# Recurrence and gated projection: values of every second head written to the other half of the PSUM partitions, block states in the scores' PSUM

## The chip, the core and the metric

The kernel runs on one core of one Trainium2 chip. The metric is the device time of one execution in microseconds (us). PE is TensorE, DVE is VectorE, ACT is ScalarE, POOL is GpSimd and SP is SyncE.

## What is computed

Four sequences, eight heads of width 48, 768 steps. Each head keeps a 48x48 state that decays per channel by `alpha` and takes in `k v`; the read-out `y = q S` of all heads, laid side by side, goes through a gated projection with a first-order recurrence.

```python
def _attn_ref(q, k, v, alpha):
    state = zeros(B, H, D, D)
    for t in range(S):
        state = alpha[:, :, t, :, None] * state + einsum('bhd,bhe->bhde', k[:, :, t], v[:, :, t])
        y[:, :, t] = einsum('bhd,bhde->bhe', q[:, :, t], state)

def _moe_ref(x, w_in, A_log, w_out):     # x: heads of y side by side, 384 wide
    val, gate = split(x @ w_in)          # 512 each
    h_t = exp(A_log)[0] * h_(t-1) + val_t
    return (silu(gate) * h) @ w_out
```

## The kernel before

The 3072 steps are worked in 12 groups of 256 steps (`GC`), three groups for each sequence. A group is two parts of 128 steps, and each part two blocks of 64 steps (`R`), so there are four blocks. Heads go in four pairs: a pair stands on 128 partitions, 64 for each head (48 padded to 64).

A generator `front(n)` brings group n in: transposes of alpha (L294, `a_pad`), scans on DVE for the decay products V (L301) and P (L306), transposes of q and k with products Q (L318) and K (L322), the scores inside each block (`sc`, L331), which DVE copies under a mask into A (L334), and transposes of K back to steps (`tpk`, L119, taken to Kn by ACT).

A generator `back(n)` makes the values of group n: `block_states` (`z`, L131) multiplies keys with values for each block, DVE adds the four block states up into S_n and, for the next group of the sequence, S_end (L356); `values_inside` (`y`, L145) multiplies the masked scores with the values, ending in a small ACT read called `fence` (L150); `values_before` (L163) adds Q times the state ahead of the block into the same PSUM; ACT copies y to `x_sb` (L363); `features` transposes it (`tpx`, L172) and ACT takes that to xT (L173).

A generator `ssm(n)` does the projection: `pj` (L93), the scan hh (L96), silu `sg` (L101), the product f (L102), and the output `o` (L107), which ACT copies out (`o_sb`, L110).

The order on every engine is written out by hand in the loop over n at the end of `ranged` (`tc.manual_schedule()`): in turn n the PE does the a transposes of group n, z of group n-1, o of group n-3, the q transposes, y inside of n-1, pj of n-2, the k transposes, y before of n-1, pj, scores, tpx, pj, tpk, pj. Engines run their own lists in order and wait for one another by semaphores. In turns 0 to 2 DVE, ACT and POOL also turn the weights from 64-bit to 32-bit numbers (L233 to L250).

The 64x64 matmuls address one quarter of the PE array each. Which quarter is set by the half of the partitions that the operands lie on (row half) and the half of the PSUM partitions that the result goes to (column half). In `block_states` the row half is the block r and the column half the head i of the pair, with result bank r. In the scores and in `values_before` the row half is i, the column half r, the bank i. In `values_inside` row half and column half are both r, the bank is i. A program matmul in fp32 shows as two PE instructions in the trace, so a block of 32 matmuls is 64 instructions there.

PSUM: `ps_sc` holds one tile of two banks (tag `sc`), `ps_y` one tile of two banks (tag `y`), which z and y take in turn; `ps_tp` and `ps_mm` hold two each.

A second function, `general`, computes the same for extreme decays and is not run with these inputs.

Of the kernel before, what the change touches and what calls it, by code (L numbers as in the profile page):

```python
# [9 lines left out]
FP32 = mybir.dt.float32  # L10
# [3 lines left out]
AF = mybir.ActivationFunctionType  # L14
# [4 lines left out]
def kernel(  # L19
# [23 lines left out]
    nc = tc.nc  # L43
    B, H, S, D = q.shape
    DM = H * D
    DI = moe_A_log.shape[0]
    C = 128
    R = 64
    NR = C // R
# [4 lines left out]
    NP = H // 2  # L54
    DP = 64
# [58 lines left out]
    def keys_back(K, Kn, ps_tp):  # L114

        for c in range(G):
            tp = ps_tp.tile([C, NP, C], FP32, tag="tp", name="tpk")
            for j in range(NP):
                nc.tensor.transpose(tp[:, j, :], K[:, j, ds(c * C, C)], ident)  # L119
            nc.scalar.activation(Kn[:, c], tp, AF.Copy)  # L120

    def block_states(Kn, v_sb, ps_y):

        z = ps_y.tile([C, NR, 512], FP32, tag="y", name="z")
        zv = z[:, :, 0:GP * D].rearrange("p r (g j e) -> p r g j e", g=G, e=D)
        for g in range(G):
            for j in range(NP):
                for r in range(NR):
                    for i in range(2):
                        rows, chs = ds(R * r, R), ds(DP * i, DP)  # L130
                        nc.tensor.matmul(zv[chs, r, g, j, :], Kn[rows, g, j, chs],  # L131
                                         v_sb[rows, g, 2 * j + i, :], start=True, stop=True,
                                         skip_group_check=True)
        return zv

    def values_inside(A, v_sb, ps_y, pool):

        y = ps_y.tile([C, 2, 512], FP32, tag="y", name="y")
        yv = y[:, :, 0:GP * D].rearrange("p i (g j e) -> p i g j e", g=G, j=NP)
        for c in range(G):  # L140
            for j in range(NP):
                for i in range(2):
                    for r in range(NR):
                        rows = ds(R * r, R)
                        nc.tensor.matmul(yv[rows, i, c, j, :], A[rows, i, c * NP + j, :],  # L145
                                         v_sb[rows, c, 2 * j + i, :],
                                         start=(c == 0 and j == 0), stop=False, skip_group_check=True)

        fence = pool.tile([C, 2, 1], FP32, name="fence")
        nc.scalar.activation(fence, y[:, :, 0:1], AF.Copy)  # L150
        return yv

    def values_before(yv, Q, S_n, first):

        for c in range(G):
            for j in range(NP):
                for r in range(NR):
                    x = c * NR + r
                    if first and x == 0:
                        continue  # L160
                    for i in range(2):
                        rows = ds(DP * i, DP)
                        nc.tensor.matmul(yv[ds(R * r, R), i, c, j, :], Q[rows, j, ds(R * x, R)],  # L163
                                         S_n[rows, x, j, :],
                                         start=False, stop=(c == G - 1 and j == NP - 1), skip_group_check=True)

    def features(x_sb, xT, ps_tp):

        for c in range(G):
            tp = ps_tp.tile([C, NK, C], FP32, tag="tp", name="tpx")  # L170
            for kk in range(NK):
                nc.tensor.transpose(tp[:, kk, :], x_sb[:, c, ds(kk * C, C)], ident)  # L172
            nc.scalar.activation(xT[:, :, ds(c * C, C)], tp, AF.Copy)  # L173
# [6 lines left out]
    def ranged(ctx):  # L180
        def pool(name, bufs, **kw):
            return ctx.enter_context(tc.tile_pool(name=name, bufs=bufs, **kw))

        own = pool("own", 1)
        p1 = pool("p1", 1)
        p2 = pool("p2", 2)
# [3 lines left out]
        ps_sc = pool("ps_sc", 1, space=PS)  # L190
        ps_tp = pool("ps_tp", 2, space=PS)
        ps_y = pool("ps_y", 1, space=PS)
# [147 lines left out]
        def back(n):  # L340

            s = st.pop(n)
            v_sb = vs.pop(n)
            first, last = n % NG == 0, n % NG == NG - 1
            S_n = p2.tile([C, GR, NP, D], FP32, name="S_n")
            if not first:
                nc.gpsimd.tensor_mul(S_n[:, 0], S_end[0], s["V"][:, :, 0:1].to_broadcast([C, NP, D]))  # L347
            zv = block_states(s["Kn"], v_sb, ps_y)
            S_end[0] = None if last else p2.tile([C, NP, D], FP32, name="S_end")
            for x in range(GR):  # L350
                src = zv[:, x % NR, x // NR]
                dst = S_n[:, x + 1] if x + 1 < GR else S_end[0]
                if first and x == 0:
                    nc.vector.tensor_copy(out=dst, in_=src)
                elif dst is not None:
                    nc.vector.tensor_add(dst, S_n[:, x], src)  # L356
            yield
            yv = values_inside(s["A"], v_sb, ps_y, p2)
            yield
            values_before(yv, s["Q"], S_n, first)  # L360
            x_sb = p2.tile([C, G, DM], FP32, name="x_sb")
            for i in range(2):
                nc.scalar.activation(x_sb.rearrange("p g (j i e) -> p i (g j) e", i=2, e=D)[:, i],  # L363
                                     yv[:, i].rearrange("p g j e -> p (g j) e"), AF.Copy)
            yield
            xs[n] = p2.tile([C, NK, GC], FP32, name="xT")
            features(x_sb, xs[n], ps_tp)
            yield
# [43 lines left out]
        with tc.manual_schedule():  # L412
            for n in range(N + 3):
                fr = front(n) if n < N else None
                ba = back(n - 1) if 0 <= n - 1 < N else None
                old, new = ssms[n - 3], None
                turn = weights if n < 3 else None
# [34 lines left out]
    def general(ctx):  # L452
# [4 lines left out]
        def pool(name, bufs, **kw):  # L457
            return ctx.enter_context(tc.tile_pool(name=name, bufs=bufs, **kw))

        LEVELS = [1, 2, 4, 8, 16, 32]  # L460
        p1 = pool("g1", 1)
        p2 = pool("g2", 2)
        ps_sc = pool("gs_sc", 1, space=PS)
        ps_tp = pool("gs_tp", 2, space=PS)
        ps_y = pool("gs_y", 1, space=PS)
# [21 lines left out]
        A = p1.tile([C, 2, GP, R], FP32, name="gA")  # L487
# [4 lines left out]
        for n in range(N):  # L492
            first = n % NG == 0
            for dst, src in (("a", alpha), ("q", q), ("k", k)):
                load_heads(pad[dst], src, n)
            v_sb = p2.tile([C, G, H, D], FP32, name="v_sb")
# [3 lines left out]
            Q = p1.tile([C, NP, GC], FP32, name="gQ")  # L500
# [22 lines left out]
            for l in LEVELS:  # L523
                nb = R // (2 * l)
                Qr = Q.rearrange("p j (x b two l) -> p j x b two l", x=GR, two=2, l=l)
                sc = ps_sc.tile([C, 2, 512], FP32, tag="sc", name="sc")
                scv = sc[:, :, 0:GP * R // 2].rearrange("p i (x b l) -> p i x b l", x=GP, l=l)
                for c in range(G):
                    for j in range(NP):
                        for r in range(NR):  # L530
                            x = c * NR + r
                            for i in range(2):
                                rows = ds(DP * i, DP)
# [19 lines left out]
            Tb = Tl.rearrange("p (j x) -> p j x", j=NP)  # L553
            Kn = p1.tile([C, G, NP, C], FP32, name="gKn")
            keys_back(K, Kn, ps_tp)
            zv = block_states(Kn, v_sb, ps_y)
            S_n = p2.tile([C, GR, NP, D], FP32, name="gS_n") if first else S_in
            S_in = p2.tile([C, GR, NP, D], FP32, name="gS_n")
            for x in range(GR):
# [4 lines left out]
                else:  # L564
                    dS = p1.tile([C, NP, D], FP32, name="gdS")
                    nc.gpsimd.tensor_mul(dS, S_n[:, x], Tb[:, :, x:x + 1].to_broadcast([C, NP, D]))
                    nc.vector.tensor_add(dst, dS, src)
            yv = values_inside(A, v_sb, ps_y, p1)
            values_before(yv, Q, S_n, first)
            x_sb = p1.tile([C, G, DM], FP32, name="gx_sb")  # L570
            for i in range(2):
                nc.vector.tensor_add(
# [10 lines left out]
    with tc.If(outside > 0):  # L583
        with ExitStack() as inner:
            general(inner)
# [30 lines left out]
```

## Time and profile before

| | |
|---|---|
| time, median of 3 runs | 373.11 us (372.81 to 375.66) |
| the profiled execution's own time | 374.53 us |
| its span, first to last instruction | 372.8 us |
| mean granted TensorE clock | 0.975 of full |
| PE busy | 325.8 us (87%) |
| DVE / ACT / POOL busy | 200.5 (54%) / 106.5 (29%) / 56.8 us (15%) |
| z, `L131`, 768 instructions | 14.6 us |
| y inside, `L145`, 768 instructions | 28.0 us |
| y before, `L163`, 704 instructions | 14.5 us |
| scores, `L331`, 768 instructions | 15.5 us |

The profile is one execution. A timeline row gives a start, a length, an engine, a line of the code, what is written from what, a count, and in square brackets how long the engine was idle before it and what ended that. An idle engine matters only where the chain of waits that ends last runs through it.

### The profile page before, as it was taken

What the parts mean: (1) busy time and instruction counts of PE and PEld (TensorE: products, weight loads), DVE (VectorE), ACT (ScalarE), POOL (GpSimd) and SP (SyncE); (2) the same over time, 40 slices, a digit from 0 to 9 for tenths busy, and PEclk for the clock granted to TensorE, in tenths of its full rate; (3) what the DMA queues carried; (4) which work ended last, traced back from release to release, by engine and by line L of the source; (5) the groups of instructions that cost most, each with busy time, mean ns of one, the idle gap of its engine ahead of it and who ended that gap; (6) DMA issues with size and microseconds to landing.
All of it is one profiled execution on the core that took longest, in us unless ns stands there. A gap on an engine that the chain in (4) does not pass through costs nothing.

```text
span 372.8 us, 9626 instructions
## 1 busy us (share of the span) xinstructions
PE 325.8 (87%) x4233; PEld 265.6 (71%) x4233; DVE 200.5 (54%) x373; ACT 106.5 (29%) x231; POOL 56.8 (15%) x77
## 2 busy tenths in 40 slices
PE   2535851899999999999999999999999999999794
PEld 1425741787887886887887887878868868878582
DVE  3939785356557438348456555565484493403140
ACT  1414354221432323133223213223332231312111
POOL 4478898510000000000000000000000000000000
PEclk9999995599999999999999999999999999999999
DMA  9999992040470740911913704607401000010101
GB/s 132 212 220 190 303 171 47 2 86 2 105 111 2 154 60 3 179 36 41 145 30 80 134 2 100 115 3 130 85 2 44 2 16 30 2 45 0 38 7 50
DMA packets 107650, 29.02 MB, mean 78 GB/s; under 512 B 100944, under 2 KB 107088, under 8 KB 107600
## 3 DMA queue, kind: packets, MB, share of 16 engines
q1 hardware_dynamic: 104992, 27.93, 40.6%
q10 hardware_dynamic: 2608, 0.40, 0.9%
q8 instruction: 35, 0.57, 0.7%
q14 instruction: 15, 0.12, 0.1%
HBM read 23.60 MB, written 4.72 MB: 76 GB/s over the span
## 4 chain that ended last, share of the span: by engine, by line
PE 62%; DVE 23%; SPq 6%; issue 4%; POOL 2%; DMA 1%; ACT 1%; ACTq 0%; DVEq 0%; POOLq 0%
PE pj L93 35%; PE y L145 7%; DVE V L301 7%; DVE P L306 7%; PE o L107 4%; SPq L83 4%; PE y L163 4%; PE sc L331 3%; PE tp L294 3%; DVE S_n L356 3%; PE tpk L119 2%; PE tpx L172 2%; SPq L226 2%; DVE hh L96 2%; DMA bits<-in_moe_w_in_dram 1%
## 5 line engine op out<-in xcount | busy, mean ns | idle before, releaser
L93 PE MATMUL pj<-xT,w_in 128*128 128x256 f32 x576 | 136.1, 388 | 0.0
L93 PEld LDWEIGHTS pj<-xT,w_in 128*128 128x128 f32 x576 | 107.7, 193 | 14.6
L96 DVE TENSOR_TENSOR_SCAN hh<-a_dec,hh,pj 128x256 f32<-128x256 f32 x32 | 23.9, 747 | 78.2 <-PE pj L93 78.2
L107 PE MATMUL o<-w_out,f 128*128 128x384 f32 x192 | 65.0, 492 | 0.0
L101 ACT ACTIVATE sg<-pj 128x256 f32<-128x256 f32 x48 | 18.4, 383 | 130.9 <-DVE hh L96 130.9
L107 PEld LDWEIGHTS o<-w_out,f 128*128 128x128 f32 x192 | 35.5, 190 | 23.0 <-DVE f L102 0.5
L145 PE MATMUL y<-v_sb,A 64*64 64x48 f32 x768 | 28.0, 233 | 11.9 <-DVE S_end L356 11.2
L347 POOL TENSOR_TENSOR S_n<-S_end,V 128x192 f32<-128x192 f32 x8 | 4.1, 513 | 224.2 <-DVE S_end L356 224.2
L145 PEld LDWEIGHTS y<-v_sb,A 64*64 64x64 f32 x768 | 26.7, 149 | 15.1 <-issue 8.3
L306 DVE TENSOR_TENSOR_SCAN P<-tp,iV,bias 128x256 f32<-128x256 f32 x48 | 33.4, 738 | 0.8
L102 DVE TENSOR_TENSOR f<-sg,hh 128x256 f32<-128x256 f32 x48 | 20.4, 426 | 23.3 <-ACT sg L101 23.3
L301 DVE TENSOR_TENSOR_SCAN V<-tp,bias 128x256 f32<-128x256 f32 x48 | 30.1, 669 | 5.1 <-PE tp L294 5.1
L96 DVE TENSOR_TENSOR_SCAN hh<-a_dec,pj 128x256 f32<-128x256 f32 x16 | 11.0, 687 | 39.4 <-PE pj L93 39.4
L311 ACT ACTIVATE junk<-V,bias 128x1024 f32<-128x1024 f32 x12 | 13.8, 1148 | 52.7 <-DVE V L301 52.7
L294 PE MATMUL tp<-ident,a_pad 128*128 128x128 f32 x96 | 14.6, 300 | 15.6 <-POOL ex L240 7.2
L294 PE MATMUL tp<-ident,q_pad 128*128 128x128 f32 x96 | 15.5, 306 | 11.9 <-DVE P L306 7.7
L294 PEld LDWEIGHTS tp<-ident,a_pad 128*128 128x128 f32 x96 | 12.4, 154 | 17.4 <-POOL ex L240 7.5
L294 PEld LDWEIGHTS tp<-ident,q_pad 128*128 128x128 f32 x96 | 12.4, 157 | 16.4 <-issue 13.8
L240 POOL TENSOR_SCALAR ex<-ex 128x384 uint32<-128x384 uint32 x12 | 18.4, 1532 | 18.0 <-DVE ex L235 17.7
L331 PEld LDWEIGHTS sc<-Q,K 64*64 64x64 f32 x768 | 13.7, 144 | 4.3 <-issue 3.3
L334 DVE COPY_PREDICATED A<-mask,sc 128x512 f32<-128x512 uint8 x24 | 16.0, 721 | 1.1 <-PE sc L331 1.1
L322 DVE TENSOR_TENSOR K<-tp,V 128x512 f32<-128x512 f32 x24 | 15.5, 684 | 2.0 <-PE tp L294 2.0
(59 smaller groups left out, 315.6 us busy)
## 6 DMA issues: line engine op xcount, KB each, us to landing
a_pad<-in_alpha_dram SPq DMA_DIRECT2D x24, 192.0 KB, 4.7
k_pad<-in_k_dram SPq DMA_DIRECT2D x24, 192.0 KB, 5.1
v_sb<-in_v_dram SPq DMA_DIRECT2D x24, 192.0 KB, 5.0
out_dram<-o_sb SPq DMA_DIRECT2D x24, 192.0 KB, 2.1
q_pad<-in_q_dram SPq DMA_DIRECT2D x22, 192.0 KB, 5.0
bits<-in_moe_w_in_dram SPq DMA_DIRECT2D x8, 384.0 KB, 5.4
bits<-in_moe_w_out_dram SPq DMA_DIRECT2D x4, 384.0 KB, 6.1
q_pad<-in_q_dram ACTq DMA_DIRECT2D x2, 192.0 KB, 5.5
```

The source lines that it names most:

```text
L93: nc.tensor.matmul(pj[:, i, :], w_in[:, kk, i, ds(cc * C, C)], xT[:, kk, :], start=(kk == 0), stop=(kk == NK - 1))
L96: nc.vector.tensor_tensor_scan(out=hh, data0=a_dec[:, cc:cc + 1].to_broadcast([C, GC]), data1=pj[:, 0, :], initial=prev_h[cc][:, GC - 1:GC ...
L101: nc.scalar.activation(sg, pj[:, 1, :], AF.Silu)
L102: nc.vector.tensor_mul(f[:, cc, :], sg, hh)
L107: nc.tensor.matmul(o, f[:, cc, ds(c * C, C)], w_out[:, cc, :], start=(cc == 0), stop=(cc == NI - 1))
L145: nc.tensor.matmul(yv[rows, i, c, j, :], A[rows, i, c * NP + j, :], v_sb[rows, c, 2 * j + i, :], start=(c == 0 and j == 0), stop=False, sk ...
L240: nc.gpsimd.tensor_scalar(out=ex, in0=ex, scalar1=896.0, scalar2=1151.0, op0=ALU.max, op1=ALU.min)
L294: nc.tensor.transpose(tp[:, u, ds(c * C, C)], pad[name][:, c, 2 * j:2 * j + 2, :], ident)
L301: nc.vector.tensor_tensor_scan(out=V[:, 2 * jj + u, GC - 1::-1], data0=tp[:, u, ::-1], data1=bias[:, 1:2].to_broadcast([C, GC]), initial=1 ...
L306: nc.vector.tensor_tensor_scan(out=P[:, 2 * jj + u, :], data0=tp[:, u, :], data1=bias[:, 1:2].to_broadcast([C, GC]), initial=iV0[:, 2 * jj ...
L331: nc.tensor.matmul(scv[ds(R * r, R), i, c * NP + j, :], K[rows, j, steps], Q[rows, j, steps], start=True, stop=True, skip_group_check=True)
L334: nc.vector.copy_predicated(out=A[:, i].rearrange("p x t -> p (x t)"), mask=mask[:, ds(i * GP * R, GP * R)], data=sc[:, i])
```

## The change

Three things are changed, all on the path of `ranged`. (1) `block_states` gets its PSUM from the pool and tag of the scores, no longer from that of y. (2) In `values_inside` and `values_before` the result of the second head of a pair (i = 1) goes to the other half of the PSUM partitions (`turn` = 1), and the loops over i and r in `values_inside` change places. In `values_inside` row half r then goes to column half r for the first head and to 1 - r for the second; the bank is still i. In `values_before` row half and bank are still i. (3) The copy of the second head to `x_sb` is done in two halves of 64 partitions, each read from the other half. `general` passes `turn` = 0.

```diff
-    def block_states(Kn, v_sb, ps_y):
+    def block_states(Kn, v_sb, pool, tag):
-        z = ps_y.tile([C, NR, 512], FP32, tag="y", name="z")
+        z = pool.tile([C, NR, 512], FP32, tag=tag, name="z")
...
-                for i in range(2):
-                    for r in range(NR):
-                        rows = ds(R * r, R)
-                        nc.tensor.matmul(yv[rows, i, c, j, :], A[rows, i, c * NP + j, :],
+                for r in range(NR):
+                    for i in range(2):
+                        rows, at = ds(R * r, R), ds(R * ((r + turn * i) % NR), R)
+                        nc.tensor.matmul(yv[at, i, c, j, :], A[rows, i, c * NP + j, :],
...
-                        rows = ds(DP * i, DP)
-                        nc.tensor.matmul(yv[ds(R * r, R), i, c, j, :], Q[rows, j, ds(R * x, R)],
+                        rows, at = ds(DP * i, DP), ds(R * ((r + turn * i) % NR), R)
+                        nc.tensor.matmul(yv[at, i, c, j, :], Q[rows, j, ds(R * x, R)],
...
-            zv = block_states(s["Kn"], v_sb, ps_y)
+            zv = block_states(s["Kn"], v_sb, ps_sc, "sc")
...
-            for i in range(2):
-                nc.scalar.activation(x_sb.rearrange("p g (j i e) -> p i (g j) e", i=2, e=D)[:, i],
-                                     yv[:, i].rearrange("p g j e -> p (g j) e"), AF.Copy)
+            nc.scalar.activation(xv[:, 0], ys[:, 0], AF.Copy)
+            for r in range(NR):
+                nc.scalar.activation(xv[ds(R * r, R), 1], ys[ds(R * (1 - r), R), 1], AF.Copy)
```

On PE, in a turn in the middle of the program, from z to the pj that follows y inside, the kernel before has (what stands in square brackets is what a row waits for):

```order
L131 MATMUL z<-v_sb,Kn 64x48 [waits DMAHW3_49]
L131 MATMUL z<-v_sb,Kn 64x48 x15
L131 MATMUL z<-v_sb,Kn 64x48 [waits DMAHW4_49]
L131 MATMUL z<-v_sb,Kn 64x48 x15
...
L294 MATMUL tp<-ident,q_pad_101 128x128 [waits DVE_49,PE_49]
L294 MATMUL tp<-ident,q_pad_101 128x128 x3
L145 MATMUL y<-v_sb,A_108 64x48 [waits DVE_49,PE_49]
L145 MATMUL y<-v_sb,A_108 64x48 x31
L93 MATMUL pj<-xT,w_in 128x256 [waits Activation_49]
```

and the changed kernel has in the same place:

```order
L131 MATMUL z<-v_sb,Kn 64x48 [waits DMAHW3_49,DVE_49]
L131 MATMUL z<-v_sb,Kn 64x48 x15
L131 MATMUL z<-v_sb,Kn 64x48 [waits DMAHW4_49]
L131 MATMUL z<-v_sb,Kn 64x48 x15
...
L295 MATMUL tp<-ident,q_pad_101 128x128 [waits DVE_49,PE_49]
L295 MATMUL tp<-ident,q_pad_101 128x128 x3
L146 MATMUL y<-v_sb,A_108 64x48 x32
L93 MATMUL pj<-xT,w_in 128x256 [waits Activation_49]
```

No instruction moved to another place in the list; y no longer waits for DVE and PE, and z waits for DVE, which reads the scores out of the PSUM that z now takes.

On ACT, from the fence to the copy of the transposed features in a turn in the middle, the kernel before has:

```order
L150 ACTIVATE fence<-y 128x2 [waits PE_49]
L101 ACTIVATE sg<-pj 128x256 [waits DVE_49]
L363 ACTIVATE x_sb<-y 128x8x48 [waits PE_49]
L363 ACTIVATE x_sb<-y 128x8x48
L101 ACTIVATE sg<-pj 128x256 [waits DVE_49]
```

and the changed kernel:

```order
L151 ACTIVATE fence<-y 128x2 [waits PE_49]
L101 ACTIVATE sg<-pj 128x256 [waits DVE_49]
L365 ACTIVATE x_sb<-y 128x8x48 [waits PE_49]
L367 ACTIVATE x_sb<-y 64x8x48 x2
L101 ACTIVATE sg<-pj 128x256 [waits DVE_49]
```

There is one ACT instruction more in each of the 12 groups, in the same place.

## Rows read from the trace of the kernel before

**Rows 1.** Page, part 1: busy time, share of span, instructions of each engine.

```profile
PE 325.8 (87%) x4233; PEld 265.6 (71%) x4233; DVE 200.5 (54%) x373; ACT 106.5 (29%) x231; POOL 56.8 (15%) x77
```

**Rows 2.** Page, part 4: the chain that ended last, shares by engine.

```profile
PE 62%; DVE 23%; SPq 6%; issue 4%; POOL 2%; DMA 1%; ACT 1%; ACTq 0%; DVEq 0%; POOLq 0%
```

**Rows 3.** Waits of PE: who waited for whom, total us, times, longest us.

```profile
PE y L145 <- DVE S_end L356: 11.2, 8, 5.4
...
PE y L145 <- DVE S_n L356: 0.7, 3, 0.2
```

**Rows 4.** Timeline, 277 to 300 us, a turn in the middle: start, length, engine, what.

```profile
277.19 1.39 DVE L306 TENSOR_TENSOR_SCAN P<-tp,iV,bias 128x256 f32<-128x256 f32 x2
...
278.40 1.04 PE L294 MATMUL tp<-ident,q_pad 128*128 128x128 f32 x8
...
279.40 0.85 ACT L110 ACTIVATE o_sb<-o 128x384 f32<-128x384 f32 x2
279.63 0.35 DVE L356 TENSOR_TENSOR S_end<-S_n,z 128x192 f32<-128x192 f32 x1
279.91 1.28 DVE L318 TENSOR_TENSOR Q<-tp,P 128x512 f32<-128x512 f32 x2
...
280.13 2.07 PE L145 MATMUL y<-v_sb,A 64*64 64x48 f32 x64 [0.69 <-DVE S_end L356]
...
284.82 1.04 PE L294 MATMUL tp<-ident,k_pad 128*128 128x128 f32 x8
...
286.97 0.87 ACT L363 ACTIVATE x_sb<-y 128x384 f32<-128x384 f32 x2 [0.78 <-PE y L163]
...
290.74 0.88 PE L172 MATMUL tpx<-ident,x_sb 128*128 128x128 f32 x6
...
291.30 1.33 DVE L334 COPY_PREDICATED A<-mask,sc 128x512 f32<-128x512 uint8 x2
...
298.47 1.15 PE L131 MATMUL z<-v_sb,Kn 64*64 64x48 f32 x64
```

**Rows 5.** The chain in order of time, two pieces: start, length, what.

```profile
285.86 1.06 PE y L163 x48
...
312.27 1.08 PE y L163 x64
```

**Rows 6.** Timeline, 30 to 47 us, the turn of group 1.

```profile
30.84 1.96 PE L131 MATMUL z<-v_sb,Kn 64*64 64x48 f32 x64
...
39.37 3.65 PE L145 MATMUL y<-v_sb,A 64*64 64x48 f32 x64 [1.60 <-DVE S_end L356]
...
46.00 1.49 POOL L240 TENSOR_SCALAR ex<-ex 128x384 uint32<-128x384 uint32 x1 [0.55 <-DVE ex L235]
```

**Rows 7.** Timeline, 50 to 76 us, the turn of group 2.

```profile
50.45 1.58 POOL L240 TENSOR_SCALAR ex<-ex 128x384 uint32<-128x384 uint32 x1 [0.30 <-DVE ex L235]
...
52.67 1.37 DVE L247 SCALAR_TENSOR_TENSOR ex<-bits,ex 128x384 uint32<-128x384 uint32 x1 [0.42 <-POOL ex L241]
...
59.78 1.09 PE L294 MATMUL tp<-ident,q_pad 128*128 128x128 f32 x4 [2.10 <-DVE P L306]
...
64.63 1.13 DVE L356 TENSOR_TENSOR S_n<-S_n,z 128x192 f32<-128x192 f32 x3 [3.71 <-POOL S_n L347]
...
66.30 3.65 PE L145 MATMUL y<-v_sb,A 64*64 64x48 f32 x64 [5.43 <-DVE S_end L356]
...
67.92 0.52 ACT L239 ACTIVATE w_out<-w_out 128x384 f32<-128x384 uint32 x1 [6.01 <-DVE w_out L237]
...
69.88 5.07 PE L93 MATMUL pj<-xT,w_in 128*128 128x256 f32 x12
...
75.75 0.45 PE L163 MATMUL y<-S_n,Q 64*64 64x48 f32 x16
```

**Rows 8.** Windows of 1 us: engines' busy us (instructions), granted clock, DMA share, GB/s.

```profile
58.00:59.00 1.00, 0.00 (x0) 0.00 (x0) 0.93 (x4) 0.90 (x1) 0.92 (x2) 0.50 0.00 0
...
75.00:76.00 1.00, 1.00 (x24) 0.83 (x26) 0.67 (x1) 0.30 (x1) 0.00 (x0) 1.00 0.00 0
```

More of the change, by code (lines that the diff above doesn't have):

```diff
@@ L134, in block_states, with values_inside @@
         return zv
-    def values_inside(A, v_sb, ps_y, pool):
+    def values_inside(A, v_sb, ps_y, pool, turn):
         y = ps_y.tile([C, 2, 512], FP32, tag="y", name="y")
@@ L151, in values_inside, with values_before @@
         return yv
-    def values_before(yv, Q, S_n, first):
+    def values_before(yv, Q, S_n, first, turn):
         for c in range(G):
@@ L357, in back @@
             yield
-            yv = values_inside(s["A"], v_sb, ps_y, p2)
+            yv = values_inside(s["A"], v_sb, ps_y, p2, 1)
             yield
-            values_before(yv, s["Q"], S_n, first)
+            values_before(yv, s["Q"], S_n, first, 1)
             x_sb = p2.tile([C, G, DM], FP32, name="x_sb")
-            for i in range(2):
-                nc.scalar.activation(x_sb.rearrange("p g (j i e) -> p i (g j) e", i=2, e=D)[:, i],
-                                     yv[:, i].rearrange("p g j e -> p (g j) e"), AF.Copy)
+            xv = x_sb.rearrange("p g (j i e) -> p i (g j) e", i=2, e=D)
+            ys = yv.rearrange("p i g j e -> p i (g j) e")
+            nc.scalar.activation(xv[:, 0], ys[:, 0], AF.Copy)
+            for r in range(NR):
+                nc.scalar.activation(xv[ds(R * r, R), 1], ys[ds(R * (1 - r), R), 1], AF.Copy)
             yield
@@ L555, in general @@
             keys_back(K, Kn, ps_tp)
-            zv = block_states(Kn, v_sb, ps_y)
+            zv = block_states(Kn, v_sb, ps_y, "y")
             S_n = p2.tile([C, GR, NP, D], FP32, name="gS_n") if first else S_in
@@ L567, in general @@
                     nc.vector.tensor_add(dst, dS, src)
-            yv = values_inside(A, v_sb, ps_y, p1)
-            values_before(yv, Q, S_n, first)
+            yv = values_inside(A, v_sb, ps_y, p1, 0)
+            values_before(yv, Q, S_n, first, 0)
             x_sb = p1.tile([C, G, DM], FP32, name="gx_sb")
```

## The prediction, made blind

> **What bounds the kernel now.** I read the busy times first: PE works 325.8 of 372.8 us and no other engine comes near [rows 1]. The chain that ended last agrees: 62% of it is PE, 23% DVE [rows 2]. DVE is in it because the PE stands still for DVE at certain places, and the waits of PE name the one that repeats: y inside a block waits for the state sums, 11.2 us in 8 times for S_end and 0.7 us in 3 for S_n [rows 3]. In a turn in the middle [rows 4] the reader is to see why. The q transposes are over at 279.44 (278.40 + 1.04). y could go on, but it takes the PSUM that z had, and DVE reads z out only behind the scans P: S_end ends at 279.98 (279.63 + 0.35), and y starts at 280.13, after 0.69 us of idle PE. Then y takes 2.07 us for 64 instructions, where z takes 1.15 for as many of the same size [rows 4]. From 282 us to the end of the turn the PE has no gap that matters, so a microsecond saved on PE there is one saved in the whole, as long as DVE and ACT still come in time.
>
> **The change part by part.**
>
> *y on four quarters.* y inside used two quarters of the array (row half = column half), z uses four. That the two quarters cause y's pace, and not something else in it, can be read from values_before: in the first group of a sequence it leaves out the first block, so that 16 of its 48 instructions have only two quarters to go to, and it takes 1.06 us where the full 64 take 1.08 [rows 5]. The 32 others cost half of 1.08, that is 0.54; the 16 cost 0.52, which is 32.5 ns each. y's pace is 2.07/64 = 32.3 ns. With four quarters it is 1.08/64 = 17 ns in values_before and 1.15/64 = 18 ns in z. The new order in y (first row half to both column halves, then the second) is that of z but for the last two of the four, so I take z's 1.15: 0.92 us less in each block. There are 12 blocks; the first two fall into the start (below), so 10 x 0.92 = 9.2 us. Bounds for the unseen pattern: from 17 ns (1.08, 0.07 better) up to y's present 32.3 ns (nothing gained) and beyond (rivals).
>
> What is new is that both row halves write both banks at a time: bank i gets row half r, and row half 1 - r in its other 64 partitions. y before already has neighbours that do so (row half 0 and row half 1 into bank i, one after the other), and runs at 32.3 ns, no slower than the 32.5 ns of values_before, whose row halves have a bank each [rows 4, 5]. So sharing a bank has no price that these rows show.
>
> The Trainium skill, TensorEngine Tiling (Array Packing), section Restrictions and Gotchas, says that different row tiles write to different PSUM banks and cannot access the same bank simultaneously. By it y would have the four quarters and still not use them at once, and the block would stay at two at a time; the trace's pair of 32.3 and 32.5 ns speaks against its biting here, though four at a time is not shown.
>
> *The wait of y.* With z in the scores' PSUM, y has no wait of its own. Of the 11.2 us, 1.60 and 5.43 belong to the first two turns with a y [rows 6, 7]; what is left is 11.2 - 1.60 - 5.43 = 4.2 us in six turns, and 0.7 in three, together 4.9 us. The twelfth y has no wait.
>
> What is late next? The sums on DVE stay where they are; PE goes ahead of them by 0.69 + 0.92 = 1.6 us a turn. pj behind y needs PSUM that ACT empties: o_sb is done at 280.25 (279.40 + 0.85), pj would start about 280.13 - 0.69 + 1.15 = 280.6, so 0.3 us are left, and more, since the first half of o_sb is enough. The k transposes need both buffers that the product Q frees at 281.19 (279.91 + 1.28); they would start at 284.82 - 1.6 = 283.2. The q transposes themselves are no closer to P than before (second half from about 278.9, P ends 278.58), since all from the last pj to there is as it was [rows 4]. So nothing takes the place of the wait; should something, its most is the 4.9 us.
>
> *The new wait of z.* z waits for the copy of the scores, which ends at 292.63 (291.30 + 1.33); z starts at 298.47 [rows 4]. 5.8 us of pj and transposes lie between. The scores in turn wait for the sums of z, over in the middle of the turn, 10 us ahead of them. Both at nothing; behind z stand o and the whole PE list, so if it waited every microsecond would count.
>
> *The copy to x_sb.* Two ACT instructions take 0.87, so 0.44 each; half the partitions at the same length cost as much, so three take 1.3. The trace shows no copy from one half of the partitions to the other; were each of the two twice as dear (0.88) it would be 2.2 us, were they half as dear there is no change. The reader of x_sb, tpx, starts 2.9 us after the copy ends (287.84 to 290.74) behind pj and the scores [rows 4]. Hidden in all these cases; without that cover it would be 0.44 x 12 = 5.3 us.
>
> *The start.* In the turn of group 2 the PE idles 5.43 us for S_end, because DVE waits for a product on POOL that stands behind the conversion of the weights [rows 7]. The granted clock is 0.50 there, the 1.2 GHz level: the PE had stood still before, and it is back at 1.00 (2.4 GHz) by 75 us, after y and a pj of 5.07 us [rows 7, 8]. Without the wait, y follows the q transposes at 59.78 + 1.09 = 60.87. The turn before is also shorter on PE (1.60 of wait and 3.65 against z's 1.96 at the low clock [rows 6]), but the scans of this turn wait for the weights' chain on POOL and DVE [rows 7], whose gaps left by DVE are 0.55 and 0.30 [rows 6, 7]; I let it come 0.85 earlier, so y at 60.0. It takes 1.96 as z did at the low clock, pj 5.07, the k transposes 1.0 [rows 4, 6, 7]: values_before could start at 68.0, where it now starts at 75.75. It also needs the fence, on ACT behind L239, which would end at 68.44 - 0.85 = 67.6, and the fence a bit later: just in time. So 7.8 us. A clock that rises earlier gives nothing more, as the fence then holds it. On the other side: no 0.85, and the low clock through the k transposes, values_before and the next pj: 1.0 for the k transposes at twice their 1.04, 0.8 by z's 1.96 for 1.15, and 2.5 for a pj at 5.07 and not half of it: 7.8 - 0.85 - 4.3 = 2.6 us.
>
> *Sum.* 9.2 + 4.9 + 7.8 = 21.9 us. The profiled execution took 374.53, that is 1.7 around its span of 372.8, and would take 352.6. The median of the runs before is 373.11, 1.4 under the profiled one; I take the sum from it: 351.2 us.
>
> **The rivals.**
>
> *y keeps its pace (the change doesn't do what it says).* Two row halves that share a bank get in each other's way, and the four quarters work two at a time. Then y stays at 2.07 and 3.65: the 9.2 are gone, the start gives 7.8 - 1.7 = 6.1, the wait 4.9. Gain 11.0, time 362.1. For it: four row and column halves crossing over two banks stand nowhere in the trace. Against it: the two equal paces above.
>
> *Slower.* Same place, worse: quarters that share a bank go strictly one after the other, each paying what a full-array transpose pays, 1.04/8 = 130 ns [rows 4]. y would take 8.3 us, 6.2 more than now in 10 blocks, less 4.9 of waits, and at the low clock about 16 us in the turn of group 2, 6 more than the gain there: about 373 + 62 - 5 + 6 = 436 us. It decides from where y's block costs more than the other gains give: (4.9 + 6.1)/12 = 0.9 us over 2.07, that is 47 ns an instruction. Against it: all 64x64 work of the trace is at 33 ns or under at full clock.
>
> *The start gives little.* The low clock lasts on or POOL's chain doesn't move: 2.6 instead of 7.8, time 356.4. For it: the clock's rise after work begins again is seen here once.
>
> *The wait comes back.* PE, 1.6 us ahead each turn, meets o_sb (0.3 us to spare) or Q: up to 4.9 lost, 356.1.
>
> **How the numbers follow.** My forecast (348.5 to 354) 0.68; the start gives little 0.12; the wait comes back 0.07; y keeps its pace 0.07; slower 0.03; better than 348.5 (a second clock dip avoided, a turn that gains more) 0.03. The range from 347 to 358 takes in the first three and leaves out the two of y and part of the last. All cases but one are faster by more than 1%, which is about what a measurement of this kernel can tell from no change: faster 0.95, within 1% 0.02 (a y at about 47 ns), slower 0.03.
>
> **What would show it.** After: y inside with 64 instructions in 1.1 to 1.2 us at full clock and its group near 15 us instead of 28.0; no wait of y for S_end; z with no wait worth naming; tpx not waiting for x_sb; a turn in the middle shorter by 1.6 us where S_end was waited for, and 1.2 where S_n was; values_before of the turn of group 2 at about 68 us. Wrong would be a y at 2 us or more, a new wait of pj or the q transposes of the size of the old one, or a clock that stays low past 70 us.

## The result, and the profile after

| | before | changed |
|---|---|---|
| time, median (the two side by side) | 373.26 us | 352.58 us (352.02 to 353.33) |
| ratio | | 0.9437, 95% interval 0.9397 to 0.9476 |
| the profiled execution's own time / span | 374.53 / 372.8 us | 352.41 / 350.7 us |
| y inside a block, 768 instructions | 28.0 us | 15.4 us |
| PE idle ahead of y inside | 11.9 us | 0.0 us |

The kernel became 20.7 us faster by the medians, 22.1 by the two profiled executions. The forecast was 351.2, in a range from 347 to 358. The ratios here and below are not quite the quotients of the two medians (here that would be 0.9446).

Page of the changed kernel, part 1 and the shares by engine of the chain that ended last (part 4):

```profile
PE 311.7 (89%) x4233; PEld 251.7 (72%) x4233; DVE 201.1 (57%) x373; ACT 113.4 (32%) x243; POOL 57.9 (17%) x77
...
PE 80%; POOL 5%; SPq 5%; DVE 3%; DMA 3%; issue 3%; ACT 0%; POOLq 0%; DVEq 0%; ACTq 0%
```

Against [rows 1, 2]: PE's busy time fell by 14 us, and DVE fell out of the chain, from 23% to 3%. The chain is PE's own work now. One row of the windows, two turns in the middle of the changed kernel (busy us and instructions of PE, PE's weight load, DVE, ACT, POOL, then the granted clock, the DMA share and GB/s), says the same:

```profile
231.00:285.00 54.00, 54.00 (x715) 42.95 (x714) 34.19 (x64) 17.80 (x39) 0.51 (x1) 1.00 0.22 46
```

PE is busy for all of the 54 us. The turn of group 10 in the timeline of the changed kernel, which answers to [rows 4]:

```profile
260.38 1.04 PE L295 MATMUL tp<-ident,q_pad 128*128 128x128 f32 x8
...
261.35 1.15 PE L146 MATMUL y<-v_sb,A 64*64 64x48 f32 x64
261.39 0.85 ACT L110 ACTIVATE o_sb<-o 128x384 f32<-128x384 f32 x2
261.62 0.35 DVE L357 TENSOR_TENSOR S_end<-S_n,z 128x192 f32<-128x192 f32 x1
261.89 1.28 DVE L319 TENSOR_TENSOR Q<-tp,P 128x512 f32<-128x512 f32 x2
...
262.43 2.86 PE L93 MATMUL pj<-xT,w_in 128*128 128x256 f32 x12
...
265.12 1.04 PE L295 MATMUL tp<-ident,k_pad 128*128 128x128 f32 x8
...
267.27 0.49 ACT L365 ACTIVATE x_sb<-y 128x384 f32<-128x384 f32 x1 [0.78 <-PE y L164]
267.77 0.98 ACT L367 ACTIVATE x_sb<-y 64x384 f32<-64x384 f32 x2
...
271.03 0.87 PE L173 MATMUL tpx<-ident,x_sb 128*128 128x128 f32 x6
...
271.59 1.33 DVE L335 COPY_PREDICATED A<-mask,sc 128x512 f32<-128x512 uint8 x2
...
278.77 1.15 PE L131 MATMUL z<-v_sb,Kn 64*64 64x48 f32 x64
```

y follows the q transposes without a gap and takes 1.15 us, as z does. S_end ends at 261.97, after y has begun. pj starts at 262.43, where the second half of o_sb ends at 262.24 (261.39 + 0.85) and the first earlier: the cover that was worked out as 0.3 us is 0.2, and it holds. z starts 5.9 us after the scores' copy (271.59 + 1.33). x_sb is ready at 268.75, 2.3 us ahead of tpx.

From the y in the turn of group 9 (236.61) to this one are 24.74 us; in the kernel before the same two starts are 26.42 apart, so 1.68 less (0.69 of wait and 0.92 of y were put in). In the turn with the S_n wait it is 25.98 and 24.74, 1.24 less.

The turn of group 2 in the changed kernel, which answers to [rows 7]:

```profile
53.49 1.26 DVE L302 TENSOR_TENSOR_SCAN V<-tp,bias 128x256 f32<-128x256 f32 x2
...
60.32 1.96 PE L146 MATMUL y<-v_sb,A 64*64 64x48 f32 x64
...
64.17 1.13 DVE L357 TENSOR_TENSOR S_n<-S_n,z 128x192 f32<-128x192 f32 x3 [3.71 <-POOL S_n L348]
...
66.34 1.25 PE L295 MATMUL tp<-ident,k_pad 128*128 128x128 f32 x8 [0.95 <-DVE Q L319]
...
67.88 0.15 ACT L151 ACTIVATE fence<-y 128x2 f32<-128x2 f32 x1
...
68.18 1.15 PE L164 MATMUL y<-S_n,Q 64*64 64x48 f32 x64 [0.58 <-ACT fence L151]
```

values_before starts at 68.18; it was 75.75, and 68.0 was forecast. Two waits stand ahead of it that the kernel before did not have there: 0.95 us of the k transposes for Q and 0.58 of values_before for the fence. In the turn of group 1 values_before has such a wait for the fence too, 0.49 us.

### The profile page after: what moved, and what is told of

Same layout as the page of the kernel before. It is cut to its first block, busy times and chain, and to the rows that moved or that the text cites. A ratio compares the mean times of both kernels' runs of the same rounds, so it can differ in the third digit from the quotient of the medians.

```text
span 350.7 us, 9637 instructions
## 1 busy us (share of the span) xinstructions
PE 311.7 (89%) x4233; PEld 251.7 (72%) x4233; DVE 201.1 (57%) x373; ACT 113.4 (32%) x243; POOL 57.9 (17%) x77
## 4 chain that ended last, share of the span: by engine, by line
PE 80%; POOL 5%; SPq 5%; DVE 3%; DMA 3%; issue 3%; ACT 0%; POOLq 0%; DVEq 0%; ACTq 0%
PE pj L93 36%; PE o L107 18%; PE tp L295 7%; SPq L83 4%; PE z L131 4%; PE y L164 3%; PE sc L332 3%; PE y L146 3%; DMA bits<-in_moe_w_in_dram 3%; PE tpk L119 2%; PE tpx L173 2%; POOL ex L241 2%; SPq L227 1%; POOL w_in L251 1%; POOL w_in L250 1%
## 5 line engine op out<-in xcount | busy, mean ns | idle before, releaser
L93 PE MATMUL pj<-xT,w_in 128*128 128x256 f32 x576 | 134.2, 384 | 0.0
L93 PEld LDWEIGHTS pj<-xT,w_in 128*128 128x128 f32 x576 | 106.2, 190 | 14.2
L102 DVE TENSOR_TENSOR f<-sg,hh 128x256 f32<-128x256 f32 x48 | 20.9, 435 | 23.8 <-ACT sg L101 23.8
L295 PE MATMUL tp<-ident,q_pad 128*128 128x128 f32 x96 | 15.4, 305 | 14.5 <-DVE P L307 7.8
L332 PE MATMUL sc<-Q,K 64*64 64x64 f32 x768 | 16.1, 237 | 0.5 <-DVE K L323 0.5
L146 PEld LDWEIGHTS y<-v_sb,A 64*64 64x64 f32 x768 | 13.8, 149 | 2.7 <-issue 2.7
L295 PE MATMUL tp<-ident,k_pad 128*128 128x128 f32 x96 | 14.5, 299 | 1.4 <-DVE Q L319 1.0
```

The lines of the kernel that those rows point to most:

```text
L93: nc.tensor.matmul(pj[:, i, :], w_in[:, kk, i, ds(cc * C, C)], xT[:, kk, :], start=(kk == 0), stop=(kk == NK - 1))
L102: nc.vector.tensor_mul(f[:, cc, :], sg, hh)
L146: nc.tensor.matmul(yv[at, i, c, j, :], A[rows, i, c * NP + j, :], v_sb[rows, c, 2 * j + i, :], start=(c == 0 and j == 0), stop=False, skip ...
L295: nc.tensor.transpose(tp[:, u, ds(c * C, C)], pad[name][:, c, 2 * j:2 * j + 2, :], ident)
L332: nc.tensor.matmul(scv[ds(R * r, R), i, c * NP + j, :], K[rows, j, steps], Q[rows, j, steps], start=True, stop=True, skip_group_check=True)
```

## Experiments

**One half of the change at a time.** The first run leaves z in the PSUM of y and keeps the rest:

```diff
-            zv = block_states(s["Kn"], v_sb, ps_sc, "sc")
+            zv = block_states(s["Kn"], v_sb, ps_y, "y")
```

> The change without its first part: z goes back to the PSUM of y, the turned columns, the loop order and the split copy stay. Theory (y's pace comes from the number of quarters, and the two gains add up): y inside takes 1.15 us a block at full clock and 1.96 at half clock as in the changed kernel, the wait for S_end and S_n is back as before (about 0.69 us in six turns, 0.24 in three, 5.4 in the turn of group 2). Time: 373.3 less 10 x 0.92 less 1.7 in the start, that is about 362.4 us. Rival (y's pace comes from the wait, its PSUM being taken over from z while z is drained): y stays near 2 us a block and the time near 373 us.

Measured: 363.11 us (ratio 0.9696, 0.965 to 0.9743), 10.4 under the runs of before beside it (373.47). PE's waits in this run (who for whom, total us, times, longest), and the turn of group 10 in its timeline:

```profile
PE y L146 <- DVE S_end L357: 11.2, 8, 5.4
...
PE y L146 <- DVE S_n L357: 0.7, 3, 0.2
```

```profile
271.69 1.15 PE L146 MATMUL y<-v_sb,A 64*64 64x48 f32 x64 [0.70 <-DVE S_end L357]
```

The time is 0.7 us above the 362.4 expected. All waits of [rows 3] are there unchanged, and y takes 1.15 with the wait in front of it. The pace does not come from the wait.

The second run moves z alone and leaves y on two quarters:

```diff
-            yv = values_inside(s["A"], v_sb, ps_y, p2, 1)
+            yv = values_inside(s["A"], v_sb, ps_y, p2, 0)
...
-            values_before(yv, s["Q"], S_n, first, 1)
+            values_before(yv, s["Q"], S_n, first, 0)
```

with the loop order of `values_inside` and the copy to x_sb as in the kernel before.

> The change without its second and third part: z in the PSUM of the scores, y as it was before on two quarters. Theory: y takes 2.07 us a block and waits for nobody; the gain is the wait of 4.9 us and 6 to 7.5 us in the start, where the fence holds values_before: time 361 to 362.5 us. Rival (the PE, ahead of DVE now, meets another wait): the 4.9 us come back as waits of pj or of the transposes, time about 366 us.

Measured: 362.96 us (ratio 0.9708, 0.9665 to 0.975), 10.5 less than before; half a microsecond above the expected stretch. In the timeline of this run y comes right behind the q transposes (267.82 + 1.04), at the old length:

```profile
268.79 2.07 PE L146 MATMUL y<-v_sb,A 64*64 64x48 f32 x64
```

Its group of instructions (busy us, mean ns of one, idle before):

```profile
L146 PE MATMUL y<-v_sb,A 64*64 64x48 f32 x768 | 28.0, 233 | 0.0
```

It is 28.0 us, as before, with no idle time ahead of it, and in the turns in the middle no other wait took the place of the one removed. In the start there is one: in the turn of group 1 tpx waits 1.38 us for x_sb, which it did not before; how much of the half microsecond that is, was not tested. The two gains, 10.4 and 10.5, sum to 20.9; the change as a whole gives 20.7. They add up, within the intervals of these runs, which are some 1.6 and 1.7 us to either side.

**Quarters or the order of neighbours.** The change altered both. The third run keeps the four quarters and takes the old loop order:

```diff
-                for r in range(NR):
-                    for i in range(2):
+                for i in range(2):
+                    for r in range(NR):
                         rows, at = ds(R * r, R), ds(R * ((r + turn * i) % NR), R)
```

> The changed kernel with the loops over i and r in values_inside in the old order (i outside, r inside); all four quarters are used, but neighbours now alternate between the row halves (0,0), (1,1), (0,1), (1,0). Theory (only the number of quarters counts): y inside stays at 1.15 us a block, time 352.6 us within 1. Rival (the order of neighbours sets the pace, as two neighbours of one row half load their weights behind one another or two row halves meet in one bank): y moves by more than 0.1 us a block, the time by more than 1 us.

Measured: 352.89 us (ratio 0.9451, 0.940 to 0.9501). The group of y inside in this run (busy us, mean ns of one, idle before):

```profile
L146 PE MATMUL y<-v_sb,A 64*64 64x48 f32 x768 | 15.4, 234 | 0.0
```

It is 15.4 us, as in the changed kernel. The fourth run is the other way round, two quarters in the new order:

> As the PSUM alone (y on two quarters, not turned), but with the new loop order in values_inside: eight PE instructions in a row alternate no more, four go to one quarter, then four to the other. Theory (the number of quarters counts, and the PE works ahead across a few instructions): y at 2.1 to 3 us a block. Rival (the PE takes them strictly in order and only neighbours overlap): near one quarter at a time, 65 ns an instruction, y at 4.1 us a block, 20 us more than with the PSUM alone, about 382 us.

Measured: 362.87 us (ratio 0.9718, 0.9672 to 0.9765), the same as the PSUM alone. The turn of group 10 in its timeline:

```profile
268.27 2.10 PE L146 MATMUL y<-v_sb,A 64*64 64x48 f32 x64
```

2.10 for 2.07, though now four instructions in a row go to one quarter. So PE does not need alternating neighbours, and the order is worth 0.03 us a block at the most: what counts is how many quarters the stretch can use.

The starts of the single instructions in these traces show what the number of quarters does. At full clock (granted 1.00) the middle of a y block goes in rounds of 58 ns. In the changed kernel four instructions start in each round (210, 217, 224 and 230 ns from the start of the block, then 269, 275, 282 and 289), and so they do in the third run. In the second run two start in each (385 and 392 ns, then 444 and 450), and in the fourth two as well (385 and 426, then 444 and 485). 64 instructions are 16 rounds or 32; the last instruction starts at 930 ns and at 1850, and with the 0.22 us that it takes itself these are the 1.15 and 2.07 us. z and values_before have the same rounds of four. What one quarter alone would take was not run.

**Is the copy to x_sb hidden, and by what?** These two runs repeat the half copies, writing the same values again:

```diff
             for r in range(NR):
                 nc.scalar.activation(xv[ds(R * r, R), 1], ys[ds(R * (1 - r), R), 1], AF.Copy)
+            for r in range(NR * 2):
+                nc.scalar.activation(xv[ds(R * (r % NR), R), 1], ys[ds(R * (1 - r % NR), R), 1], AF.Copy)
```

> The changed kernel with the two half copies to x_sb made three times (the same values into the same place): four more ACT instructions of 0.49, 1.96 us a turn, 23.5 us of ACT work in all. In the changed kernel x_sb is ready 2.28 us ahead of its reader tpx in a turn in the middle (268.75 to 271.03). Theory (the copy lies under pj and the scores): time within 1 us of 352.6, at most 2 us more from the first and last turns, where the cover is thinner. Rival (ACT is near its bound through what waits behind the copy): 5 us or more slower.

Measured: 354.06 us (353.39 to 354.17). With `NR * 4` in place of `NR * 2`:

> As the run before, but the half copies five times: eight more ACT instructions, 3.92 us a turn. Now the cover of 2.28 us is used up: theory: tpx waits about 1.65 us for x_sb in each of the nine turns in the middle, about 2 in the first and last, so 352.6 + 15 to 20 = 368 to 373 us. Rival (there is more cover than the gap to tpx): under 360 us.

Measured: 379.31 us (378.82 to 380.48), ratio 1.0158 (1.0135 to 1.0181): slower than the kernel before. PE's waits, first of the run with four more copies, then of that with eight:

```profile
PE tpx L173 <- ACT x_sb L369: 3.3, 2, 2.4
```

```profile
PE tpx L173 <- ACT x_sb L369: 25.3, 12, 4.2
```

and a turn in the middle of the latter:

```profile
265.88 0.88 PE L173 MATMUL tpx<-ident,x_sb 128*128 128x128 f32 x6 [1.81 <-ACT x_sb L369]
```

23.5 us of ACT work cost 1.5 us, and tpx waited for it only twice, in no turn of the middle (2.39 us in the turn of group 1, 0.88 in the last). Twice as much used up the cover, as expected, but the 379.3 lie above the expected 368 to 373. Each turn in the middle waits 1.78 to 1.81 us (1.65 was expected), and the three outer ones 4.19, 2.03 and 2.91, together 9.1, more than the 2 each that I had put in; 352.6 + 25.3 is 378, and the last 1.4 us are not accounted for. So the change's own third copy, 5.9 us of ACT work in 12 turns, is free in the turns of the middle because of the pj and the scores ahead of tpx, with room for four more and not for eight.

**What holds the start.** In the changed kernel the turn of group 2 still waits in two places: the k transposes 0.95 us for Q on DVE, values_before 0.58 for the fence on ACT. Both stand behind the weights' work in the order written for that turn. This run changes that order in the one turn:

```diff
-                step(turn)
-                step(ba)
+                for g in ((ba, turn) if n == 2 else (turn, ba)):
+                    step(g)
```

at the first two places of the loop.

> The changed kernel with one thing moved: in the turn of group 2 the first two steps of back (z with the state sums, and y inside with its fence) come ahead of the weights' steps in the written order, no longer behind them. So POOL's product for S_n stands ahead of one weight unit, and the fence ahead of that unit's ACT work. Theory (in the changed kernel the start is held by DVE's sums waiting for POOL, and by the fence behind ACT's weight work: k transposes waited 0.95 us for Q, values_before 0.58 for the fence): both waits go, values_before starts near 66.4 instead of 68.2, and the time falls by 1.5 to 1.9 us, to about 351.0. Rival (the weights' chain on POOL or the clock holds the start anyway): within 0.5 us of 352.6.

Measured: 351.29 us (351.21 to 353.02), 1.3 under the changed kernel, but measured apart from it. Side by side:

> The run with the state sums first once more, beside the changed kernel on one chip. Theory (the two waits in the start are gone for good): 1.3 us under the changed kernel, 351.3. Rival (the difference was of the chips): the same as the changed kernel within 0.4.

> The changed kernel itself once more, beside the two others on one chip, so that differences of 1 us can be told: 352.6 us within 0.5.

Measured: 351.91 us (351.02 to 352.46; ratio to before 0.9407) and 352.74 us (352.28 to 353.04; ratio 0.9433): 0.8 less by the medians of six executions each, whose ranges overlap by 0.2 us. 1.3 was expected, so this lies between the theory and the rival. The start of the turn in the timelines of the two, first the changed kernel again, then the one with the state sums first:

```profile
53.39 1.26 DVE L302 TENSOR_TENSOR_SCAN V<-tp,bias 128x256 f32<-128x256 f32 x2
...
62.12 4.77 PE L93 MATMUL pj<-xT,w_in 128*128 128x256 f32 x12
...
68.10 1.15 PE L164 MATMUL y<-S_n,Q 64*64 64x48 f32 x64 [0.33 <-ACT fence L151]
```

```profile
54.06 1.26 DVE L302 TENSOR_TENSOR_SCAN V<-tp,bias 128x256 f32<-128x256 f32 x2
...
62.80 3.82 PE L93 MATMUL pj<-xT,w_in 128*128 128x256 f32 x12
62.93 0.17 ACT L151 ACTIVATE fence<-y 128x2 f32<-128x2 f32 x1 [0.60 <-PE y L146]
...
67.42 1.15 PE L164 MATMUL y<-S_n,Q 64*64 64x48 f32 x64
```

The fence is 5 us earlier and the wait gone, but in this execution the scans V came 0.67 later, from work ahead of them that the edit does not touch: z of the turn before starts at 30.73 for 30.11, and ahead of it ACT's first step on a block of weights, which waits for their transfer, at 26.83 for 26.20. From V to values_before it is 14.71 us in the one and 13.36 in the other, 1.35 less. What is left is PE's own work at the clock it gets: pj takes 3.82 here, and took 4.42 in the first profile of this edit, where it is 13.95 from V to values_before, 0.74 less than the 14.69 of the first profile of the changed kernel. The granted clock (the third number from the end in these rows of the windows) in 64 to 66 us was 0.80 here and 0.50, the 1.2 GHz level, there:

```profile
64.00:66.00 2.00, 2.00 (x9) 1.69 (x8) 2.00 (x3) 0.85 (x2) 1.88 (x2) 0.80 0.07 14
```

```profile
64.00:66.00 2.00, 2.00 (x7) 1.55 (x6) 2.00 (x3) 0.84 (x2) 1.89 (x2) 0.50 0.11 21
```

The theory that the fence and Q held the start is borne out, its size of 1.5 to 1.9 was too large.

**The step that holds the scans.** V in that turn stands on DVE behind the last weights' step of the turn before, which waits for POOL. This run leaves that step for the turn of group 2, in addition to the last edit:

```diff
-                step(turn)
+                step(turn if n != 1 else None)
                 step(new)
                 if n == N:
```

> The run with the state sums first, and in addition the weights' step at the end of the turn of group 1 is left for the turn of group 2 (its four remaining steps all have a place there). In the changed kernel the scans V of the turn of group 2 start at 53.49, held on DVE by that step, which waits 1.40 us for POOL; the a transposes were over at 49.95. Theory (the start is held by the weights' chain on POOL through DVE's order): V starts near 50.2, all behind it 2.5 to 3.3 us earlier, time 348.0 to 349.0 us, if w_out is still ready for o in the next turn. Rival (the last of w_in on POOL, at 54.42, or the clock holds pj anyway, or w_out comes late for o): within 0.5 us of the run with the state sums first, about 351.3 us.

Measured, beside the last two: 348.04 us (347.54 to 348.36), ratio to before 0.9308 (0.9284 to 0.9331), 4.7 under the changed kernel and 3.9 under the state sums first. In its timeline:

```profile
49.80 1.27 DVE L302 TENSOR_TENSOR_SCAN V<-tp,bias 128x256 f32<-128x256 f32 x2 [0.36 <-PE tp L295]
...
63.26 1.15 PE L164 MATMUL y<-S_n,Q 64*64 64x48 f32 x64
```

V waits for the a transposes and no longer for the weights; values_before starts at 63.26, 4.8 us earlier than in the changed kernel (68.10), about the gain of the whole, and the time is in the expected 348.0 to 349.0. In the start the copy to x_sb is no longer hidden: tpx waits 1.14 us for it in the turn of group 1 and 0.38 in the next. This version beats both kernels; it is the change plus an order of the weights' steps in two turns.

## Why the prediction was right, step by step

*What bounds.* Right: PE, and where PE stood still, the waits that the rows named. With these waits gone, DVE left the chain.

*y on four quarters, 0.92 us a block.* Right to the hundredth: 1.15 us, z's length. That y's pace came from two quarters was read off values_before in [rows 5]; the runs with one half of the change and with the loop orders changed show it, and so do the rounds of 58 ns with two starts or four. The rival in which row halves that share a bank get in each other's way is out: in y both row halves write both banks, in either order, and the block takes what z takes, where each row half has a bank to itself. By the Trainium skill, TensorEngine Tiling (Array Packing), section Restrictions and Gotchas, different row tiles cannot access the same bank simultaneously; the 1.15 us of y show no cost of it here, where the two write different halves of the partitions of that bank. Two row halves in the same half of the partitions of one bank at once were not tried.

*The wait of y, 4.9 us.* Right: no wait of y in the changed kernel, and the turns in the middle shorter by what the sum of wait and y gave (1.68 and 1.24 us), even by some 0.07 us more. Nothing took its place there; the narrow one, o_sb ahead of pj, held with 0.2 us.

*The new wait of z and the copy to x_sb, both at nothing.* Right, 5.9 us and 2.3 us of cover. The half copy, read from the other half of the partitions, takes 0.49 us, the same as a whole one in place, so the three take 1.5 us, a little more than the 1.3 put in. A half copy in place was not run, so what the crossing alone costs was not measured.

*The start, 7.8 us.* Right in size, wrong in one term, and partly by luck. The 0.85 us by which I let POOL's chain come earlier did not come. V started at 53.49 for 53.96, but z of the turn before started at 30.21 for 30.84 [rows 6], so the whole execution was already 0.63 earlier there, ahead of anything that the change can reach. In the twelve profiles of this case that z starts anywhere from 30.11 to 31.05 us. In this pair the difference is there at ACT's first step on a block of weights, which waits for their transfer (26.31 for 26.93). Counted from V, values_before comes at 14.69 us in the changed kernel and at 21.79 before: 7.1 us. So the 68.18, so near to the 68.0, owes 0.47 us to an execution that was early. What led to it differs too: I had PE's own work at the low clock, with the fence just in time; in the profile PE was faster than that and waited for Q and for the fence. The gap of 0.55 on POOL [rows 6] did close, and the two POOL operations ahead of it became longer. In the timelines, before and after:

```profile
43.36 1.02 POOL L249 TENSOR_TENSOR w_in<-w_in,bits 128x384 f32<-128x384 f32 x1
44.10 0.69 DVE L322 TENSOR_TENSOR K<-tp,V 128x512 f32<-128x512 f32 x1 [1.87 <-PE tp L294]
44.45 1.00 POOL L250 TENSOR_TENSOR w_in<-w_in,ex 128x384 f32<-128x384 f32 x1
```

```profile
42.80 1.20 POOL L250 TENSOR_TENSOR w_in<-w_in,bits 128x384 f32<-128x384 f32 x1
...
43.51 0.90 DVE L248 SCALAR_TENSOR_TENSOR ex<-bits,ex 128x384 uint32<-128x384 uint32 x1
...
44.08 1.20 POOL L251 TENSOR_TENSOR w_in<-w_in,ex 128x384 f32<-128x384 f32 x1
```

That took up 0.38 of the 0.55. In the changed kernel DVE's step L248 on the weights (43.51 to 44.41) runs beside both of them. In the kernel before DVE was waiting for PE for most of the first, and the second ran beside the K product and took 1.00 all the same. So the longer time goes with that step and not with the K product; that it is the cause was not tested.

The clock gave nothing, as forecast: pj of that turn took 4.77 us in the second profile of the changed kernel, and 3.18 in the first, and values_before started at 68.10 and 68.18. The granted clock in 62 to 64 us, second profile and first:

```profile
62.00:64.00 2.00, 2.00 (x13) 1.55 (x10) 0.00 (x0) 0.00 (x0) 1.92 (x3) 0.50 0.58 115
```

```profile
62.00:64.00 2.00, 2.00 (x19) 1.69 (x14) 0.00 (x0) 0.00 (x0) 1.92 (x3) 0.77 0.66 129
```

What PE gained by the higher level it gave back waiting for Q and the fence: 0.95 and 0.58 us in the first, 0 and 0.33 in the second. In the run with the state sums first, where these waits are gone, pj's length counts.

*The sum.* 9.2 + 4.9 + 7.8 = 21.9 against 22.1 in the profiled executions, but errors met in that. The start is 7.1 by the change, and 0.5 more came from the execution of before being late ahead of it, which is no gain of the change. From values_before of that turn to the end of the span it is 297.05 us before and 282.52 after: 14.5, where 9.2 + 4.9 = 14.1 was put in. 7.1 + 0.5 + 14.5 is 22.1. Against the medians the 21.9 is 1.2 us too much (20.7). The start was 0.7 too high and the rest 0.4 too low, so the terms explain only 0.3 of it. Where the other 0.9 lies no trace shows: the terms were read from a profiled execution of the kernel before that was 1.3 us above the median (374.53 for 373.26), and only the late start of 0.5 can be seen in it. The wait that comes back, y at its old pace, the slower case: none occurred.

## What to carry to other kernels

In this kernel a 64x64 matmul was paid by how many quarters the stretch around it could use (at full clock 1.15 us for 64 instructions with four, 2.07 to 2.10 with two), not by the order of neighbours; another block of the same kernel that happened to use two of four told the price ahead of time. Two results that take turns in one PSUM buffer put the reader of the first on the path of the second, even where the engine in between has much time to spare; look for a buffer whose user is done by then. After both, the next thing to look at is the order of side work on the engines that feed the path: here two steps moved in two turns were worth another 4.7 us.

## What the runs showed that was not expected

Four instructions in a row to one quarter cost hardly more than alternating ones (2.10 us a block for 2.07). Either PE reached past them to the other quarter, or one quarter alone can start two in a round of 58 ns; the records do not say which quarter an instruction went to, and no run used one quarter alone. And a copy of 64 partitions from one half to the other took as long as a copy of 128 in place (0.49 us each).
